# Batch 0's attention by pairs of tiles in a fused attention and expert kernel

## The chip, the cores and the metric

The kernel runs on one core of a Trainium2 chip. The metric is the device time of one execution in microseconds, the median of several runs. PE is the matrix engine, DVE the vector engine, ACT the scalar engine, POOL the GpSimd engine, SP the engine that issues most DMAs.

## The reference

Three layers follow each other. The attention has 2 batches, 8 heads, 576 positions and 64 columns a head; scores below the row's maximum less `tau` are masked:

```python
scores = scale * np.matmul(q, k.transpose(0, 1, 3, 2))
thresh = np.max(scores, axis=-1, keepdims=True) - tau
scores = np.where(scores >= thresh, scores, -1000000000.0)
scores = scores - np.max(scores, axis=-1, keepdims=True)
attn = np.exp(scores)
attn = attn / (np.sum(attn, axis=-1, keepdims=True) + 1e-09)
return np.matmul(attn, v).astype(np.float32)
```

Its output, as 1152 tokens of 512 columns, goes through `h = max(x @ w1, x @ w2, x @ w3)` and `h @ w_out` (the inner width is 768), and then through four experts of width 1024, each `relu(x @ w1[e]) @ w2[e]`, added up with normalised weights from `domain_probs`. The weights of the middle layer arrive as 64-bit floats, all else as 32-bit floats.

## The kernel before

All products are made in a 32-bit format of PE that keeps fewer bits, so each operand is split into a high part (a rounded copy, mostly on ACT) and a low part (the rest, on DVE or POOL), and two or three products are added up.

*Stages.* Batch 0's attention comes first (`attention_fast`, L408 to L473). The middle layer and the experts for the first 512 tokens follow (`layer_max(0)`, `experts(0)`), with batch 1's attention (`attention_slow`, L475) woven in from about 180 us; then the same layers for the other tokens. All their matmuls stand at L771.

*Tiles.* Batch 0 has four jobs, one for each pair of heads. Each job has nine tiles (`job_steps`, L208): four chunks of 128 query rows for either head, and one remainder tile with the 64 last rows of both heads. The two tiles of a chunk share a buffer `em` (L251), whose halves are the exponentials of either head; `st.mate` of the second tile is the first.

*One tile.* `qk` (L228) makes the scores with matmuls at L243 into a buffer of two PSUM banks; there are two such buffers. `peak` (L249) takes the negated maximum on DVE (L254). `limit` (L256) makes the threshold, one column on DVE (L257). `power` (L259) makes the exponential on ACT (L261). `weigh` (L263) masks it on DVE and adds it up at once (L266); this frees the score buffer. `norm` (L269) adds 1e-9 to the sum (L272), takes the reciprocal (L273), both one column on DVE, and scales the tile by it on POOL, for the last tiles on DVE (L274). `turn` (L280) transposes the tile on PE (L284, for some tiles L287 too). `cut_hi` (L307) and `cut_lo` (L323) split it: by turns with a second transposition on PE and a subtraction there (L330, L337, L338) or with a copy for POOL (L314, L334, L335), for remainders and the last tiles on DVE (L340). After half a job `gather` (L348) multiplies by the values (L360) and splits the result into X (L374, L377).

*Pipeline.* The loop of `attention_fast` goes tile by tile. In one turn tile i passes through `peak`, `power`, `limit` and `weigh`, tile i+1 through `qk`, tile i-1 through `norm` and `turn`, and tile i-2 through the splits. `advance` lets two queues make one step each: the preparation of the next job (`prep`, L130) and the value products.

*Order.* In batch 0's attention the order on each engine is not written out: a planner takes what is ready by its own times, earlier calls first. From the middle layer on, PE, DVE, ACT and POOL keep the order of the calls (`ORDER_B`, "pdas"). The first three weight blocks of the middle layer are prepared in the gaps of the attention (L584 to L604, then L564 and L568). `SWIFT` says for how many of the last tiles `norm` runs on DVE, `CALM` for how many the split is DVE's.

Of the kernel before, what the change touches and what calls it, by code (L numbers as in the profile page):

```python
# [14 lines left out]
ALU = mybir.AluOpType  # L15
# [6 lines left out]
def fused_kernel(ctx: ExitStack, tc: tile.TileContext, q, k, v, tau, w1, w2, w3, w_out, probs, m_w1, m_w2, out):  # L22
# [28 lines left out]
    LOAD, CUT = 1.5, 0.25  # L51
    AFTER = 1000
    EARLY = 3
    SWIFT = 2
    QUE0 = 3072
    QUE1 = 3072
    QUE2 = 10000
    CALM = 3
    DUP = nc.scalar.copy
    ORDER_A = ""  # L60
    ORDER_B = "pdas"
# [47 lines left out]
    def atile(shape, dt, tag):  # L109
        return at["pool"].tile(shape, dt, tag=tag, name=tag, bufs=at["bufs"].get(tag, 1))  # L110
# [138 lines left out]
    def peak(st):  # L249

        st.em = st.mate.em if st.mate else atile([P, 2 * S], F32, "em")  # L251
        st.col = (st.h or 0) * S
        st.stat = {x: atile([P, 1], F32, f"st_{x}") for x in ("negm", "thr", "sum", "r")}
        nc.vector.tensor_reduce(out=st.stat["negm"], in_=views(st)[0], op=ALU.max, axis=AX.XY, negate=True)  # L254

    def limit(st):  # L256
        nc.vector.tensor_scalar(out=st.stat["thr"], in0=st.stat["negm"], scalar1=-1.0, scalar2=ntau, op0=ALU.mult, op1=ALU.add)  # L257

    def power(st):  # L259
        sv, _, ev = views(st)  # L260
        nc.scalar.activation(out=ev, in_=sv, func=AF.Exp, bias=st.stat["negm"])  # L261

    def weigh(st):  # L263

        sv, _, ev = views(st)
        nc.vector.scalar_tensor_tensor(  # L266
            out=ev, in0=sv, scalar=st.stat["thr"], in1=ev, op0=ALU.is_ge, op1=ALU.mult, accum_out=st.stat["sum"])

    def norm(st, swift=False):  # L269
        em = views(st)[1]  # L270
        su, re = st.stat["sum"], st.stat["r"]
        nc.vector.tensor_scalar(out=su, in0=su, scalar1=1e-9, scalar2=None, op0=ALU.add)  # L272
        nc.vector.reciprocal(out=re, in_=su)  # L273
        last = (nc.vector if swift else nc.gpsimd).tensor_scalar(out=em, in0=em, scalar1=re, scalar2=even, op0=ALU.mult, op1=ALU.add)  # L274
        if st.h is None:
            nc.gpsimd.tensor_scalar(
                out=st.em[:, S:S + REM], in0=st.em[:, MAIN:S], scalar1=1.0, scalar2=1.0, op0=ALU.mult, op1=ALU.mult)
        return last
# [120 lines left out]
    def lined_up(jobs):  # L399
        steps = []  # L400
        for j, job in enumerate(jobs):
            new = job_steps(job)
            for r, st in enumerate(new):
                st.job, st.j, st.r = job, j, r
            steps += new
        return steps

    def attention_fast(jobs, modes):  # L408

        steps = lined_up(jobs)  # L410
        n = len(steps)
        front, back = Queue(), Queue()
        load_job(jobs[0])
        front.add(prep(jobs[0]))
        front.drain()
        back.add(values(jobs[0]))

        def advance():
            front.advance()
            back.advance()  # L420

        urgent = ExitStack()
        for i in range(n + 3):
            st = steps[i] if i < n else None
            nxt = steps[i + 1] if i + 1 < n else None
            old = steps[i - 2] if 0 <= i - 2 < n else None
            if st and st.j + 1 < len(jobs):
                if st.r == LOAD_A:
                    load_job(jobs[st.j + 1])
                if st.r == PREP_A:  # L430
                    front.add(prep(jobs[st.j + 1]))
            if i == 0:
                qk(st)
            if st:
                peak(st)
            if 0 <= i - 1 < n - 1:
                norm(steps[i - 1], i - 1 >= n - SWIFT)
            if nxt:
                if nxt.r == 0:
                    front.drain()  # L440
                    back.add(values(nxt.job))
                qk(nxt)
            if st and not nxt:
                power(st)
                limit(st)
                weigh(st)
                at["normed"] = norm(st, True)
                turn(steps[i - 1])
                urgent.enter_context(tc.issue_after(at["normed"].ins))
            if old:  # L450
                cut_hi(old, next(modes) if old.h is not None and i - 2 < n - CALM else "dve")
            advance()
            if nxt:
                power(st)
            if old:
                cut_lo(old)
            if nxt:
                limit(st)
            advance()
            if nxt:  # L460
                weigh(st)
                if i:
                    turn(steps[i - 1])
            if st and not nxt:
                at["turned"] = turn(st)
            if old:
                cut_late(old)
                if old.last:
                    back.add(gather(old.grp, i - 2 == n - 1))
            advance()  # L470
            yield
        back.drain()
        urgent.close()  # L473

    def attention_slow(jobs, modes):  # L475
# [12 lines left out]
        for i in range(n + 1):  # L488
# [30 lines left out]
            advance()  # L519
            yield  # L520
            if st:
                norm(st)
            if old:
                cut_lo(old)
# [386 lines left out]
```

## Time and profile before

| | |
|---|---|
| median of 3 runs | 750.08 us (749.97 to 750.29) |
| the profiled execution | 751.23 us |
| its span, first to last instruction | 749.4 us |
| mean granted TensorE clock | 1.000 |
| DMA, mean over the span | 92 GB/s |

The rows are read so. Times are in microseconds, means of one instruction in ns. PE is matmuls, PEld the weight loads that overlap them. A wait names the engine and line that waited, and the line whose end released it; idle time of an engine that does not set the pace costs nothing. Matmul ends are modelled, so that neighbours overlap in the listing.

### The profile page before, as it was taken

To read this page: it belongs to the slowest core of one execution; us is meant where nothing else is said; L and a number is where in the kernel's file an instruction comes from. 1 tells how busy PE (TensorE), PEld (TensorE's weight loads), DVE (VectorE), ACT (ScalarE), POOL (GpSimd) and SP (SyncE) were. 2 spreads that over 40 slices of the span, in tenths; PEclk is the share of its full clock that TensorE was granted. 3 is DMA by queue.
4 is the path that set the end of the run, shared out by engine and by line. 5 is a ranking of instruction groups with operands and counts; after the bars stand their busy time and mean duration, and the time that the engine had idled before them with its cause. 6 is when DMAs were issued, how large, how long until landed. Compare 5 with 4: busy or idle time off the path is not lost.

```text
span 749.4 us, 11712 instructions
## 1 busy us (share of the span) xinstructions
PE 714.0 (95%) x4103; PEld 634.9 (85%) x4103; DVE 378.6 (51%) x894; ACT 345.4 (46%) x740; POOL 396.2 (53%) x438
## 2 busy tenths in 40 slices
PE   3698999999999999999999999999999999999997
PEld 3587898777788788888888899999998998998996
DVE  3898897776365765766766421112222222222222
ACT  6598885445555555565464413324421321321320
POOL 5789884776755555564564525544623523522520
PEclk9999999999999999999999999999999999999999
DMA  6601004876723224122212233213412312312303
GB/s 184 197 18 33 0 2 126 277 229 211 194 84 90 58 70 118 57 73 57 84 58 65 77 113 86 67 54 92 128 56 84 96 46 85 106 44 77 113 2 71
DMA packets 81051, 68.95 MB, mean 92 GB/s; under 512 B 15840, under 2 KB 67040, under 8 KB 80992
## 3 DMA queue, kind: packets, MB, share of 16 engines
q1 hardware_dynamic: 80960, 68.19, 31.3%
q8 instruction: 33, 0.54, 0.3%
q14 instruction: 26, 0.21, 0.1%
q0 software_dynamic: 32, 0.00, 0.0%
HBM read 59.53 MB, written 8.65 MB: 91 GB/s over the span
## 4 chain that ended last, share of the span: by engine, by line
PE 77%; DVE 7%; POOL 4%; ACT 4%; issue 3%; DMA 3%; SPq 1%; POOLq 0%; ACTq 0%; DVEq 0%
PE ps L771 63%; PE u L360 4%; PE s L243 4%; PE t L284 3%; POOL a L568 2%; DVE st_negm L254 1%; DVE em L266 1%; ACT em L261 1%; DVE raw L604 1%; PE u L159 1%; DMA krem<-in_k_dram 1%; DMA words<-in_moe_w_dram 1%; ACT a L564 1%; POOL b L596 1%; DMA raw<-in_moe_w_dram 1%
## 5 line engine op out<-in xcount | busy, mean ns | idle before, releaser
L568 POOL TENSOR_TENSOR a<-raw,a 128x512 fp32r<-128x512 f32 (+1 forms) x116 | 145.3, 1259 | 162.8 <-ACT a L564 159.4
L771 PE MATMUL ps<-b,hh 128*128 128x512 f32 x576 | 184.4, 392 | 0.0
L771 PEld LDWEIGHTS ps<-b,hh 128*128 128x128 f32 x576 | 107.3, 188 | 20.6
L721 ACT ACTIVATE hh<-ps 128x320 fp32r<-128x320 f32 (+1 forms) x96 | 46.9, 489 | 151.1 <-PE ps L771 150.8
L771 PE MATMUL ps<-b,hl 128*128 128x512 f32 x288 | 113.1, 393 | 0.0
L771 PE MATMUL ps<-y1h,a 128*128 128x320 f32 x512 | 112.8, 309 | 0.0
L568 POOL TENSOR_TENSOR b<-raw,b 128x512 fp32r<-128x512 f32 x64 | 83.0, 1299 | 52.0 <-ACT b L564 52.0
L724 DVE SCALAR_TENSOR_TENSOR hl<-ps,hh 128x320 fp32r<-128x320 f32 (+1 forms) x96 | 53.5, 557 | 106.0 <-ACT hh L721 105.9
L564 ACT ACTIVATE a<-raw 128x512 fp32r<-128x512 f32 (+1 forms) x116 | 69.6, 612 | 58.6 <-PE ps L771 22.2
L740 DVE SCALAR_TENSOR_TENSOR acc<-ps,pr,acc 128x512 f32<-128x512 f32 x63 | 47.1, 748 | 80.4 <-PE ps L771 80.3
L261 ACT ACTIVATE em<-s,st_negm 128x576 f32<-128x576 f32 x72 | 53.5, 744 | 70.5 <-DVE st_negm L254 70.1
L771 PEld LDWEIGHTS ps<-y1h,a 128*128 128x128 f32 x512 | 85.7, 188 | 0.3
L771 PE MATMUL ps<-y0h,a 128*128 128x512 f32 x256 | 84.1, 399 | 1.2 <-POOL a L568 1.2
L274 POOL TENSOR_SCALAR em<-em,st_r,even 128x576 f32<-128x576 f32 x70 | 58.8, 841 | 47.0 <-DVE st_r L273 44.3
L771 PE MATMUL ps<-y1l,a 128*128 128x320 f32 x256 | 79.1, 309 | 0.0
L254 DVE TENSOR_REDUCE st_negm<-s 128x1 f32<-128x576 f32 x72 | 54.1, 753 | 48.8 <-PE s L243 48.4
L243 PE MATMUL s<-K,QS 128*128 128x288 f32 x320 | 59.5, 314 | 9.0 <-DVE em L266 8.4
L266 DVE SCALAR_TENSOR_TENSOR em<-s,st_thr,em 128x576 f32<-128x576 f32 x72 | 58.3, 812 | 11.9 <-ACT em L261 7.9
L771 PE MATMUL ps<-x1h,a 128*128 128x320 f32 x288 | 63.4, 309 | 0.0
L771 PEld LDWEIGHTS ps<-b,hl 128*128 128x128 f32 x288 | 54.1, 188 | 9.8
L243 PEld LDWEIGHTS s<-K,QS 128*128 128x128 f32 x320 | 49.6, 197 | 14.8 <-issue 7.0
L771 PEld LDWEIGHTS ps<-y0h,a 128*128 128x128 f32 x256 | 47.0, 188 | 9.9 <-POOL a L568 1.6
(109 smaller groups left out, 1280.5 us busy)
## 6 DMA issues: line engine op xcount, KB each, us to landing
raw<-in_moe_w_dram SPq DMA_DIRECT2D x128, 256.0 KB, 2.9
words<-in_moe_w_dram SPq DMA_DIRECT2D x18, 512.0 KB, 6.8
kept_w<-raw SPq DMA_DIRECT2D x18, 256.0 KB, 2.7
raw<-kept_w SPq DMA_DIRECT2D x18, 256.0 KB, 2.7
words<-in_moe_w_out_dram SPq DMA_DIRECT2D x8, 384.0 KB, 3.6
qraw<-in_q_dram SPq DMA_DIRECT2D x8, 256.0 KB, 3.5
kraw<-in_k_dram SPq DMA_DIRECT2D x16, 128.0 KB, 3.7
vraw<-in_v_dram SPq DMA_DIRECT2D x8, 256.0 KB, 3.7
```

The source lines that it names most:

```text
L243: nc.tensor.matmul(st.s[:, kh, 0:HS], lhsT=l, rhs=r, start=i == 0, stop=i == len(terms) - 1)
L254: nc.vector.tensor_reduce(out=st.stat["negm"], in_=views(st)[0], op=ALU.max, axis=AX.XY, negate=True)
L261: nc.scalar.activation(out=ev, in_=sv, func=AF.Exp, bias=st.stat["negm"])
L266: nc.vector.scalar_tensor_tensor(out=ev, in0=sv, scalar=st.stat["thr"], in1=ev, op0=ALU.is_ge, op1=ALU.mult, accum_out=st.stat["sum"])
L274: last = (nc.vector if swift else nc.gpsimd).tensor_scalar(out=em, in0=em, scalar1=re, scalar2=even, op0=ALU.mult, op1=ALU.add)
L360: at["valued"] = nc.tensor.matmul(pv, lhsT=l, rhs=r, start=i == 0, stop=i == len(terms) - 1)
L564: nc.scalar.activation(out=b["hi"], in_=b["raw"], func=AF.Copy)
L568: nc.gpsimd.tensor_tensor(out=b["lo"], in0=b["raw"], in1=f32(b["hi"]), op=ALU.subtract)
L721: nc.scalar.activation(out=hs[f][0][:, a:z], in_=ps, func=AF.Relu)
L724: nc.vector.scalar_tensor_tensor(out=hs[f][1][:, a:z], in0=ps, scalar=0.0, in1=f32(hs[f][0][:, a:z]), op0=ALU.max, op1=ALU.subtract)
L740: nc.vector.scalar_tensor_tensor(out=accs[t], in0=ps, scalar=pe, in1=accs[t], op0=ALU.mult, op1=ALU.add)
L771: nc.tensor.matmul(ps, lhsT=l, rhs=r, start=i == 0, stop=i == count - 1)
```

## The change

The loop goes by units: the two tiles of a chunk, or a remainder alone. The statistics of a pair lie in one tile of two columns. Both tiles of a unit pass through `peak` and `power`; one `limit` covers both columns; then `weigh` of either tile, mixed with `turn` and the splits of the unit before and with `qk` of the next unit; one `invert` (the sum and the reciprocal, taken out of `norm`) for both; then `norm` of either. `SWIFT` and `CALM` count units. `attention_slow` calls `invert` for each tile.

```diff
--- before.py
+++ after.py
@@ -51,11 +51,11 @@
     LOAD, CUT = 1.5, 0.25
     AFTER = 1000
     EARLY = 3
-    SWIFT = 2
+    SWIFT = 1
     QUE0 = 3072
     QUE1 = 3072
     QUE2 = 10000
-    CALM = 3
+    CALM = 2
     DUP = nc.scalar.copy
     ORDER_A = ""
     ORDER_B = "pdas"
@@ -250,11 +250,14 @@
 
         st.em = st.mate.em if st.mate else atile([P, 2 * S], F32, "em")
         st.col = (st.h or 0) * S
-        st.stat = {x: atile([P, 1], F32, f"st_{x}") for x in ("negm", "thr", "sum", "r")}
+
+        st.both = st.mate.both if st.mate else {x: atile([P, 2], F32, f"st_{x}") for x in ("negm", "thr", "sum", "r")}
+        st.stat = {x: t[:, st.h or 0:(st.h or 0) + 1] for x, t in st.both.items()}
         nc.vector.tensor_reduce(out=st.stat["negm"], in_=views(st)[0], op=ALU.max, axis=AX.XY, negate=True)
 
-    def limit(st):
-        nc.vector.tensor_scalar(out=st.stat["thr"], in0=st.stat["negm"], scalar1=-1.0, scalar2=ntau, op0=ALU.mult, op1=ALU.add)
+    def limit(st, both=False):
+        x = {nm: t[:, 0:2] for nm, t in st.both.items()} if both else st.stat
+        nc.vector.tensor_scalar(out=x["thr"], in0=x["negm"], scalar1=-1.0, scalar2=ntau, op0=ALU.mult, op1=ALU.add)
 
     def power(st):
         sv, _, ev = views(st)
@@ -266,11 +269,14 @@
         nc.vector.scalar_tensor_tensor(
             out=ev, in0=sv, scalar=st.stat["thr"], in1=ev, op0=ALU.is_ge, op1=ALU.mult, accum_out=st.stat["sum"])
 
+    def invert(st, both=False):
+        x = {nm: t[:, 0:2] for nm, t in st.both.items()} if both else st.stat
+        nc.vector.tensor_scalar(out=x["sum"], in0=x["sum"], scalar1=1e-9, scalar2=None, op0=ALU.add)
+        nc.vector.reciprocal(out=x["r"], in_=x["sum"])
+
     def norm(st, swift=False):
         em = views(st)[1]
-        su, re = st.stat["sum"], st.stat["r"]
-        nc.vector.tensor_scalar(out=su, in0=su, scalar1=1e-9, scalar2=None, op0=ALU.add)
-        nc.vector.reciprocal(out=re, in_=su)
+        re = st.stat["r"]
         last = (nc.vector if swift else nc.gpsimd).tensor_scalar(out=em, in0=em, scalar1=re, scalar2=even, op0=ALU.mult, op1=ALU.add)
         if st.h is None:
             nc.gpsimd.tensor_scalar(
@@ -407,8 +413,13 @@
 
     def attention_fast(jobs, modes):
 
-        steps = lined_up(jobs)
-        n = len(steps)
+        units = []
+        for st in lined_up(jobs):
+            if st.mate:
+                units[-1].append(st)
+            else:
+                units.append([st])
+        n = len(units)
         front, back = Queue(), Queue()
         load_job(jobs[0])
         front.add(prep(jobs[0]))
@@ -419,55 +430,53 @@
             front.advance()
             back.advance()
 
+        def begin(st):
+            if st.r == 0:
+                front.drain()
+                if st.j:
+                    back.add(values(st.job))
+            qk(st)
+
         urgent = ExitStack()
-        for i in range(n + 3):
-            st = steps[i] if i < n else None
-            nxt = steps[i + 1] if i + 1 < n else None
-            old = steps[i - 2] if 0 <= i - 2 < n else None
-            if st and st.j + 1 < len(jobs):
-                if st.r == LOAD_A:
-                    load_job(jobs[st.j + 1])
-                if st.r == PREP_A:
-                    front.add(prep(jobs[st.j + 1]))
-            if i == 0:
-                qk(st)
-            if st:
+        for st in units[0]:
+            begin(st)
+        for i in range(n + 1):
+            new = units[i] if i < n else []
+            nxt = units[i + 1] if i + 1 < n else []
+            old = units[i - 1] if i else []
+            for st in new:
+                if st.j + 1 < len(jobs):
+                    if st.r == LOAD_A:
+                        load_job(jobs[st.j + 1])
+                    if st.r == PREP_A:
+                        front.add(prep(jobs[st.j + 1]))
                 peak(st)
-            if 0 <= i - 1 < n - 1:
-                norm(steps[i - 1], i - 1 >= n - SWIFT)
-            if nxt:
-                if nxt.r == 0:
-                    front.drain()
-                    back.add(values(nxt.job))
-                qk(nxt)
-            if st and not nxt:
                 power(st)
-                limit(st)
-                weigh(st)
-                at["normed"] = norm(st, True)
-                turn(steps[i - 1])
+                advance()
+            if new:
+                limit(new[0], len(new) == 2)
+            for k in range(2):
+                if k < len(old):
+                    at["turned"] = turn(old[k])
+                    cut_hi(old[k], next(modes) if old[k].h is not None and i - 1 < n - CALM else "dve")
+                advance()
+                if k < len(new):
+                    weigh(new[k])
+                if k < len(nxt):
+                    begin(nxt[k])
+                if k < len(old):
+                    cut_lo(old[k])
+                    cut_late(old[k])
+                    if old[k].last:
+                        back.add(gather(old[k].grp, i == n))
+                advance()
+            if new:
+                invert(new[0], len(new) == 2)
+            for st in new:
+                at["normed"] = norm(st, i >= n - SWIFT)
+                advance()
+            if i == n - 1:
                 urgent.enter_context(tc.issue_after(at["normed"].ins))
-            if old:
-                cut_hi(old, next(modes) if old.h is not None and i - 2 < n - CALM else "dve")
-            advance()
-            if nxt:
-                power(st)
-            if old:
-                cut_lo(old)
-            if nxt:
-                limit(st)
-            advance()
-            if nxt:
-                weigh(st)
-                if i:
-                    turn(steps[i - 1])
-            if st and not nxt:
-                at["turned"] = turn(st)
-            if old:
-                cut_late(old)
-                if old.last:
-                    back.add(gather(old.grp, i - 2 == n - 1))
-            advance()
             yield
         back.drain()
         urgent.close()
@@ -519,6 +528,7 @@
             advance()
             yield
             if st:
+                invert(st)
                 norm(st)
             if old:
                 cut_lo(old)
```

## Rows read from the trace of the kernel before

**Rows 1.** Busy us by stage: engines, granted clock, DMA share, GB/s.
```profile
13.00:40.00 27.00, 17.04 (x95) 14.81 (x94) 23.68 (x61) 18.82 (x43) 19.32 (x25) 1.00 0.61 179
40.00:118.50 78.50, 71.74 (x533) 65.44 (x533) 69.20 (x228) 66.89 (x153) 64.56 (x90) 1.00 0.05 13
118.50:180.00 61.50, 58.08 (x280) 47.65 (x279) 48.47 (x85) 30.59 (x60) 44.08 (x49) 1.00 0.73 229
```

**Rows 2.** PE's waits from 13 to 40 us: total, times, longest.
```profile
PE s L243 <- DVE em L266: 7.2, 4, 3.6
```

**Rows 3.** PE's waits from 40 to 118.5 us.
```profile
PE t L284 <- POOL em L274: 2.2, 4, 1.0
PE s L243 <- DVE em L266: 1.2, 2, 0.9
PE t L284 <- ACT am L338: 1.0, 1, 1.0
```

**Rows 4.** PE's waits from 118.5 to 200 us.
```profile
PE ps L771 <- POOL a L568: 3.1, 5, 1.2
```

**Rows 5.** Groups by line and shape, 0 to 118.5 us: busy, mean ns, idle before.
```profile
L266 DVE SCALAR_TENSOR_TENSOR em<-s,st_thr,em 128x576 f32<-128x576 f32 x36 | 29.0, 811 | 5.9 <-ACT em L261 3.3 <-POOL K L179 1.6 <-POOL VR L197 0.6
L274 POOL TENSOR_SCALAR em<-em,st_r,even 128x576 f32<-128x576 f32 x34 | 29.0, 854 | 9.7 <-DVE st_r L273 7.1 <-DVE st_thr L257 1.8 <-PE t L284 0.5
...
L254 DVE TENSOR_REDUCE st_negm<-s 128x1 f32<-128x576 f32 x36 | 26.8, 748 | 2.1 <-PE s L243 1.8
...
L257 DVE TENSOR_SCALAR st_thr<-st_negm,ntau 128x1 f32<-128x1 f32 x36 | 7.1, 204 | 0.2
...
L273 DVE RECIPROCAL st_r<-st_sum 128x1 f32<-128x1 f32 x36 | 5.5, 153 | 0.2
...
L272 DVE TENSOR_SCALAR st_sum<-st_sum 128x1 f32<-128x1 f32 x36 | 5.2, 144 | 0.3
...
L266 DVE DVE_READ_ACCUMULATOR em<-s,st_thr,em 128x1 f32 x36 | 2.9, 82 | 0.0
...
L342 DVE TENSOR_TENSOR ar<-u,ar 64x64 fp32r<-64x64 f32 x8 | 1.7, 217 | 0.1
```

**Rows 6.** DVE in order of time: start us, duration us, line, operation.
```profile
87.70 0.14 DVE L272 TENSOR_SCALAR st_sum<-st_sum 128x1 f32<-128x1 f32 x1
87.77 0.81 DVE L266 SCALAR_TENSOR_TENSOR em<-s,st_thr,em 128x576 f32<-128x576 f32 x1
...
93.08 0.21 DVE L257 TENSOR_SCALAR st_thr<-st_negm,ntau 128x1 f32<-128x1 f32 x1
93.20 0.15 DVE L273 RECIPROCAL st_r<-st_sum 128x1 f32<-128x1 f32 x1
93.27 0.41 DVE L340 TENSOR_TENSOR am<-t,am 128x256 fp32r<-128x256 f32 x1
```

**Rows 7.** L257 alone by stretch: DVE busy us and count.
```profile
13.00:40.00 27.00, 1.76 (x9) 1.00 0.61 179
40.00:109.00 69.00, 5.11 (x27) 1.00 0.05 14
```

**Rows 8.** All engines in order of time, the end of the attention stage.
```profile
108.51 0.78 PE L243 MATMUL s<-K,QS 128*128 128x288 f32 x4
...
113.07 0.58 DVE L274 TENSOR_SCALAR em<-em,st_r,even 128x576 f32<-128x576 f32 x1
...
115.00 0.60 PE L284 MATMUL t<-ident,em 128*128 128x128 f32 x4
...
118.22 0.31 PE L360 MATMUL u<-ar,VR 128*128 128x320 f32 x1
```

**Rows 9.** L243 alone by stretch: PE and weight-load busy us.
```profile
40.00:109.00 69.00, 21.71 (x119) 16.77 (x120) 1.00 0.05 14
```

**Rows 10.** L243 in the stage: duration ns least, median, greatest.
```profile
L243 PE MATMUL s<-K,QS x160: 289/295/607, 11.4 to 109.0; 128*128 128x288 f32 x160
```

## The prediction

> **What bounds the kernel now.** I read the table by stage first [rows 1]. The reader is to see three stretches. From 13 to 40 us DVE is busy 23.68 of 27.00 us and PE only 17.04. From 40 to 118.5 us, the rest of batch 0's attention, PE is busy 71.74 of 78.50 us and DVE (69.20), ACT (66.89) and POOL (64.56) follow closely: PE sets the pace there, but no engine has much room. After 118.5 us come the dense layers, where PE is busy 58.08 of 61.50 us in the first part. So the change, which touches only what happens before 118.5 us, can win at most what PE idles there.
>
> Next I read who ends PE's idle time. Between 13 and 40 us it is above all DVE: the score matmuls at L243 wait 7.2 us for `weigh` (L266) to free a score buffer [rows 2]. Between 40 and 118.5 us the listed waits come to 6.6 us: 2.2 us for `norm` on POOL, 1.2 us for `weigh`, and 3.2 us in six smaller items, the greatest 1.0 us, for ACT and others that the change does not speed up [rows 3]. So 3.4 of 6.6 us, about half, hang on the DVE chain and the `norm` behind it.
>
> Last I looked at what comes after: the greatest of PE's waits from 118.5 to 200 us, 3.1 us, is for split weights on POOL [rows 4]. Order on PE, DVE, ACT and POOL is written out there, so that stage starts when attention lets go of the engines.
>
> **The small instructions.** Batch 0 has 36 tiles: 32 in 16 pairs and 4 remainders. Each tile has one L257, one L272 and one L273, 36 of each, with means of 204, 144 and 153 ns [rows 5]. A pair now issues one of each, so 16 of each kind go, 48 in all. By recorded durations that is 16 x (204 + 144 + 153) ns = 8.0 us. But these records overlap their followers: an L272 starts at 87.70 us and the next DVE instruction at 87.77; an L273 at 93.20 and the next at 93.27; an L257 at 93.08 and the next at 93.20 [rows 6]. By these distances one of each costs 0.07 + 0.07 + 0.12 = 0.26 us, and the 48 cost 4.2 us of DVE time. I take 4.2, because what the follower can use is the distance between starts, and keep 8.0 for the end of the range. Where the follower needs the result the full duration counts, so the truth lies between.
>
> The Trainium skill ("VectorE: DVE Perf Modes", section "The DRAIN you can't avoid") says that the next VectorE instruction does not start until the pipe has emptied, and its rules for kernel authors advise to cut the number of instructions. The trace does not agree with the strict form: a recorded 0.14 us stood for 0.07 us of issue in the row above. By the strict form the saving would be the 8.0 us; that case is a rival below.
>
> No row shows these three on two columns. The nearest wider row is L342 on 64 columns, 217 ns [rows 5]: about what L257 takes on one column, so at the near end a second column costs nothing; at the far end it costs the 73 ns by which L342 exceeds L272, and the 60 instructions that are left (20 units, three each) would give back 4.4 us. I take nothing.
>
> **Where the saving lands.** Of the 36 L257, 9 lie between 13 and 40 us and the others after it [rows 7]. A quarter of 4.2 us is 1.05 us in the first stretch, where PE waits for DVE; DVE is busy 88% of it, so I count 0.9 us. Three quarters, 3.15 us, fall where PE is the pace; of the waits about half hang on this chain, so I count half, 1.6 us. The other half only makes DVE idle longer.
>
> **What the pair adds as waits.** (1) The threshold of tile 0 now waits for the maximum of tile 1 (0.75 us), and `norm` of tile 0 for `weigh` of tile 1 (0.81 + 0.08 us) [rows 5]. Behind the waiting threshold DVE holds both `weigh`; behind these PE holds the next score matmuls, since there are two score buffers and the pair takes both. The loop through one buffer is: two maxima 1.50, threshold 0.20, first `weigh` 0.89, score matmuls 0.78 [rows 5, 8], together 3.37 us. In the stage a pair takes 69.0 / 27 x 2 = 5.1 us [rows 7], so 1.7 us are left for DVE's other work (splits and sums of other tiles) before this loop is the pace. The exponential of tile 0 is hidden behind the maximum of tile 1, that of tile 1 behind the first `weigh`. While DVE goes round, PE has 71.74 - 21.71 = 50.0 us of other work [rows 1, 9] over some 28 tiles, 3.6 us a pair, against a hole of 1.84 us (maximum of tile 1, threshold, `weigh`) between the second score product and the next first. On average that covers it. (2) POOL does two `norm` in a row, and the turns come one unit later, behind the next pair's maxima; PE waited for `norm` four times already (2.2 us) [rows 3]. Growing each by 0.89 us would be 3.6 us; I take 0.3, since the new place of the turns leaves at least the two maxima (1.5 us) for POOL's two `norm` of 0.85 us [rows 5]. Below nothing is possible too: four waits less are -2.2.
>
> **The end of the stage.** In the last two tiles nothing of substance changes but the pairing: both are normalised on DVE and split on DVE before and after (two tiles or one unit; the third from last is a remainder, which is always split there). Now the last `norm` ends at 113.65 us and its turn begins at 115.00, held by matmuls ahead of it on PE [rows 8]. That is 1.35 us of cover for a pair's delay of about 0.9 us (the first `weigh` behind the last maximum). I take 0.2; without the cover it is 0.9.
>
> **The rest.** Batch 1's attention issues the same instructions as before; only their columns lie in a shared tile: nothing. Loads and preparation are called a little earlier in a unit: their DMAs stay far from the limit between 40 and 118.5 us (DMA share 0.05 [rows 1]), nothing, up to 0.5 either way at the start, where the share is 0.61. From 118.5 us on I pass on the whole gain, since the written order there just starts earlier; at least 0.7 of it would pass if the weight chain, which makes PE wait 3.1 us, held its own time.
>
> **Sum.** -0.9 - 1.6 + 0.3 + 0.2 = -2.0 us. The profiled execution took 751.23 us (749.4 span and 1.83 around it), so a profiled one would take 749.2; the median of the runs, 750.08, lies 1.15 us lower, and the same step from there is **748.1 us**. With the bounds (half the saving, or none lost to pairing) this case's own range is 746.5 to 749.3.
>
> **Rivals.**
> (a) *The pair starves PE* (slower). The hole of 1.84 us must be filled by turns in pairs that have no value product (L360) beside them. Two turns and a second transposition are at most 3 x 0.60 us [rows 8], 1.8 us, and DVE's other work can stretch the hole by up to the 1.7 us left above. That is a bubble of nothing to 1.7 us on the 8 pairs without a value product, up to 14 us; at 0.8 us each it is 6.4, less the 2.5 saved, +3.9: 754.0 us. It decides once the hole grows past some 2.1 us, where 8 bubbles of 0.3 us eat the 2.5 us. For it: PE already waited for `weigh`, up to 0.9 us at a time, after 40 us [rows 3]. Against: the average cover is twice the hole.
> (b) *No change.* DVE is not the pace after 40 us; the saving becomes DVE idle time and only the first stretch gains, 0.9 less 0.5: 749.7 us. For it: the 6.6 us of waits are spread over POOL, ACT and DVE. Against: half of them end with the chain that gets shorter.
> (c) *The full durations count*: 8.0 us, a quarter of it (2.0) and half of the rest (3.0) less 0.5: -4.5, 745.6 us. The strict rule of the Trainium skill above would bring this; the starts 0.07 us apart speak against it.
> (d) *The columns are not independent*: the second maximum, which writes the tile that the first exponential reads, waits for it (0.75 us [rows 5]) in all 16 pairs, half of it hidden: +6 - 2 = 754 us. The halves of `em` already are written by different engines side by side, so I give it little.
> (e) *The new order disturbs the start*: weight conversion fills DVE gaps there, and PE's score products take up to 607 ns there against 295 in the median, at a granted clock of 1.00 [rows 1, 10], so that its first matmuls may quicken earlier or later: 2 us either way.
>
> **How the numbers follow.** Likeliest case 0.45, (a) 0.20, (b) 0.17, (c) 0.10, (d) 0.04, (e) 0.04. The time is the likeliest's. About 0.2% (1.5 us) is what can be told from no change, so faster is below 748.6. Faster: four fifths of the likeliest, (c), half of (e) and a little of (b): 0.50. Within: 0.24. Slower: (a), (d) and half of (e): 0.26. The range runs from 745.0, which holds (c), to 753.0, which leaves out the upper half of (a) and (d).
>
> **What would show it.** 20 of each small instruction before the stage ends; the last value product (L360, now ending at 118.5 us [rows 8]) about 2 us earlier, nearly half of it by 40 us; PE waits on `norm` and `weigh` together below 3.4 us. Rival (a) shows as L243 waiting for L266 by well over 1.2 us after 40 us; (b) as DVE idle up and PE idle unchanged; (d) as second maxima waiting for ACT. The prediction is wrong if the stage ends later, or if it ends earlier and the waits on L568 after it grow by as much.

## The result and the profile after

The changed kernel took **756.2 us** (median of 4 runs, 754.54 to 757.24) against 750.1 us (749.97 to 750.29): ratio 1.0079, 95% interval 1.0062 to 1.0095. It is slower by about 5.9 us where the prediction had 2.0 us faster. The 5.9 us are the ratio's; the medians are 6.1 us apart. The profiled execution of after is its shortest run, 754.54 us with a span of 752.8 us, and that of the kernel before took 751.23 us, longer than any of its four runs here, so the rows below hold 3.3 us of the loss.

The table by stage for after, with the columns of [rows 1]:

```profile
13.00:40.00 27.00, 17.71 (x97) 14.82 (x96) 23.40 (x50) 19.59 (x46) 20.84 (x27) 0.94 0.63 184
40.00:118.50 78.50, 68.23 (x497) 60.97 (x498) 69.95 (x183) 63.09 (x145) 63.02 (x87) 1.00 0.03 9
118.50:180.00 61.50, 57.92 (x288) 48.09 (x289) 48.12 (x84) 30.92 (x61) 41.65 (x46) 1.00 0.71 215
```

Two things stand here. From 40 to 118.5 us PE does 3.5 us less work than before (68.23 against 71.74). And DVE, which lost 48 instructions, is no less busy: 69.95 us against 69.20. The groups by line and shape, 0 to 122 us, tell why [rows 5]:

```profile
L269 DVE SCALAR_TENSOR_TENSOR em<-s,st_thr,em 128x576 f32<-128x576 f32 x36 | 28.7, 815 | 3.4 <-ACT em L264 2.0
L280 POOL TENSOR_SCALAR em<-em,st_r,even 128x576 f32<-128x576 f32 x34 | 28.2, 838 | 8.4 <-DVE st_r L275 6.9 <-PE t L290 0.9 <-PE u L168 0.5
L260 DVE TENSOR_SCALAR st_thr<-st_negm,ntau 128x2 f32<-128x2 f32 x16 | 7.2, 449 | 0.3
L274 DVE TENSOR_SCALAR st_sum<-st_sum 128x2 f32<-128x2 f32 x16 | 5.7, 357 | 0.2
L275 DVE RECIPROCAL st_r<-st_sum 128x2 f32<-128x2 f32 x16 | 2.6, 160 | 0.3
```

The reciprocal of two columns costs what that of one did (160 against 153 ns). The threshold went from 204 to 449 ns and the sum from 144 to 357 ns: 32 instructions take 12.9 us where 32 narrow ones took 5.6. Merging removed 48 records and made 32 of the others 7.3 us longer in all.

The timeline of after shows what they wait for (start us, duration us, engine, line, operation, idle time before):

```profile
91.58 1.29 POOL L341 TENSOR_TENSOR am<-tcopy,am 128x512 fp32r<-128x512 f32 x1
91.76 1.14 DVE L274 TENSOR_SCALAR st_sum<-st_sum 128x2 f32<-128x2 f32 x1
92.93 0.17 DVE L275 RECIPROCAL st_r<-st_sum 128x2 f32<-128x2 f32 x1
93.20 1.63 POOL L280 TENSOR_SCALAR em<-em,st_r,even 128x576 f32<-128x576 f32 x2 [0.33 <-DVE st_r L275]
94.08 0.66 PE L290 MATMUL t<-ident,em 128*128 128x128 f32 x4 [1.17 <-POOL em L280]
```

The sum starts while POOL's L341 runs and ends at 92.90 us, 0.03 us after L341 does (92.87). Of its 1.14 us the `norm` loses little: POOL was busy with L341 until 92.87 us in any case and then sat idle for 0.33 us before the `norm`, so no more than 0.33 of the 1.17 us that PE waits here can be the hold's. What the hold takes for certain is time of DVE.

The hold shows nearly throughout. Of the 16 two-column sums, the eight that began with POOL idle took 0.15 to 0.17 us; of the eight begun while POOL ran, seven ended 0.02 to 0.03 us after POOL's instruction and took 0.28 to 1.14 us, and the eighth began 0.01 us before POOL's ended. Of the 16 two-column thresholds thirteen ended 0.02 to 0.03 us after an instruction of POOL; one, at 100.18 us, took 0.23 us while a `norm` that POOL had begun 0.08 us before it ran on for another 0.53 us. In the kernel before, one-column ones that began while POOL ran took 0.19 to 0.22 us (threshold) and 0.14 to 0.15 us (sum), no longer than the others. No semaphore asks for the wait, and the profile counts it as busy time.

The Trainium skill ("SBUF — State Buffer", section "Who interferes with whom") says that VectorE and GpSimd share one pair of ports into SBUF, that a `tensor_scalar` can enter a two-port mode, and that the second to start is then blocked until the first is done. This trace agrees, with the ends above, but for that one threshold. The prediction did not draw on it.

PE's waits in after, from 13 to 40 us [rows 2]:

```profile
PE u L149 <- ACT kraw L138: 3.3, 1, 3.3
PE u L293 <- DVE K L176: 2.2, 1, 2.2
PE s L243 <- DVE em L269: 1.5, 1, 1.5
```

From 40 to 118.5 us [rows 3]:

```profile
PE t L290 <- POOL em L280: 4.0, 5, 1.2
PE s L243 <- DVE em L269: 1.2, 3, 0.6
PE t L290 <- DVE em L280: 0.9, 1, 0.9
```

And from 118.5 to 200 us [rows 4]:

```profile
PE ps L781 <- POOL a L578: 2.3, 5, 0.5
```

In the first stretch the wait for `weigh` fell as foreseen, from 7.2 to 1.5 us, and waits of the next job's preparation (L149, L293) took its place. After 40 us the scores wait for `weigh` no more than before (1.2 us); the turns wait for `norm` twice as long (4.0 against 2.2 us, and 0.9 us for the last one on DVE). The dense layers give back 0.8 us.

The end of the stage in after [rows 8]:

```profile
111.64 0.80 PE L243 MATMUL s<-K,QS 128*128 128x288 f32 x4
...
116.82 1.53 DVE L280 TENSOR_SCALAR em<-em,st_r,even 128x576 f32<-128x576 f32 x2
117.60 0.63 PE L290 MATMUL t<-ident,em 128*128 128x128 f32 x4 [0.90 <-DVE em L280]
...
122.53 0.31 PE L366 MATMUL u<-ar,VR 128*128 128x320 f32 x1
```

The last score matmuls start at 111.64 us instead of 108.51, 3.1 us late, and the last value product ends at 122.84 instead of 118.53: the tail adds 1.2 us to what was lost ahead of it. Where it was lost shows in PE's busy time in three stretches of the stage (window, length, busy us, count, granted clock, DMA share, GB/s), for the kernel before:

```profile
20.00:40.00 20.00, 13.32 (x82) 1.00 0.56 166
40.00:90.00 50.00, 44.83 (x334) 1.00 0.07 19
90.00:118.50 28.50, 26.91 (x202) 1.00 0.01 2
```

and for after:

```profile
20.00:40.00 20.00, 14.46 (x86) 0.91 0.60 180
40.00:90.00 50.00, 44.48 (x328) 1.00 0.05 13
90.00:118.50 28.50, 23.75 (x171) 1.00 0.01 1
```

Until 90 us after is level; in the last 28.5 us it does 31 matmul records less. The last matmul of a job's preparation starts at 88.0 us in the kernel before and at 87.1 us in after, so in those 28.5 us no preparation fills PE's gaps.

### The profile page after: what moved, and what is told of

It is laid out like the page before. It is cut to its first block, busy times and chain, and to the rows that moved or that the text cites. A ratio compares the mean times of both kernels' runs of the same rounds, so it can differ in the third digit from the quotient of the medians.

```text
span 752.8 us, 11646 instructions
## 1 busy us (share of the span) xinstructions
PE 715.5 (95%) x4103; PEld 634.7 (84%) x4103; DVE 382.7 (51%) x846; ACT 345.1 (46%) x740; POOL 396.7 (53%) x438
## 4 chain that ended last, share of the span: by engine, by line
PE 75%; DVE 10%; POOL 4%; issue 4%; ACT 3%; DMA 2%; SPq 0%; DVEq 0%; POOLq 0%; ACTq 0%
PE ps L781 63%; PE u L366 4%; PE s L243 4%; PE t L290 2%; DVE st_negm L256 2%; DVE em L269 2%; POOL a L578 2%; DMA words<-in_moe_w_dram 1%; DMA kraw<-in_k_dram 1%; PE u L159 1%; DVE raw L614 1%; POOL b L606 1%; DVE x L371 1%; ACT a L574 1%; ACT em L264 1%
## 5 line engine op out<-in xcount | busy, mean ns | idle before, releaser
L243 PE MATMUL s<-K,QS 128*128 128x288 f32 x320 | 59.1, 314 | 3.3 <-DVE em L269 2.7
L243 PEld LDWEIGHTS s<-K,QS 128*128 128x128 f32 x320 | 49.8, 198 | 8.7 <-DVE em L269 4.6
```

The costliest lines, as they stand in the source:

```text
L243: nc.tensor.matmul(st.s[:, kh, 0:HS], lhsT=l, rhs=r, start=i == 0, stop=i == len(terms) - 1)
```

## The experiments

Two theories to begin with. **A**: the two-column `tensor_scalar`, held by POOL, costs the time. **B**: working in pairs, or the new order of work that comes with it, costs it. All ratios are to the kernel before, run on the same chip beside them. Where "order fixed" is said, the order of the instructions on every engine is written out as that of the changed kernel; elsewhere the planner makes an order of its own, and that need not be the order of the calls.

**e2_wide.** The kernel before, tile by tile, in nearly its own order (13 of 4103 matmul records stand elsewhere in its trace), with threshold and sum on two columns; the second is a dummy.

```
-out=st.stat["thr"], in0=st.stat["negm"]   # [P, 1]
+out=st.wide["thr"], in0=st.wide["negm"]   # [P, 2]; the sum likewise
```

> The kernel before, tile by tile, but threshold and sum work on two columns (the second is a dummy that nothing reads), 72 instructions. Theory A: each is held by 0.23 us in the mean as in the changed kernel, 16 us of DVE time, half of it on the path: 754 to 762 us. Theory B: nothing that starves PE is added, 750 to 751.

Measured: 760.01 us, ratio 1.0127 [1.0114, 1.0141]. Its two groups, and its stage from 40 to 118.5 us:

```profile
L269 DVE TENSOR_SCALAR rg_thr<-rg_negm,ntau 128x2 f32<-128x2 f32 x36 | 20.1, 567 | 0.2
L285 DVE TENSOR_SCALAR rg_sum<-rg_sum 128x2 f32<-128x2 f32 x36 | 12.3, 341 | 0.3
```

```profile
40.00:118.50 78.50, 67.66 (x486) 59.58 (x485) 75.41 (x209) 63.55 (x143) 61.01 (x86) 1.00 0.05 12
```

Width alone, with no instruction merged and no pair, costs 9.5 us: DVE goes from 69.20 to 75.41 us and PE loses 4.1 us of work, as theory A had it. The hold costs time here.

**p1_narrow, p3_all, p4_reduce.** The changed kernel, order fixed, with the hold taken away: p1 makes threshold and sum per tile (32 instructions more), p3 the reciprocal too (48 more), p4 keeps one instruction per pair but makes threshold and sum as `tensor_reduce` over a value and a constant.

```
-limit(new[0], len(new) == 2)          # p1, p3: one column each
+for st in new: limit(st)
-tensor_scalar(out=thr[:, 0:2], ...)   # p4
+tensor_reduce(out=thr[:, 0:2], in_=(negm, -ntau)[:, 0:2, :], op=add, negate=True)
```

> The first round mixed two things, since the planner made a new order for each kernel. Here every engine keeps the order of the changed kernel, instruction for instruction (written out as edges between neighbours); only the threshold and the sum of a pair are two one-column instructions, one behind the other. Theory A (the hold of the two-column form is on the path): 3 to 6 us below the changed kernel's 756.2, 750 to 753 us. Theory B (the order and the pairing cost the time, the hold is hidden): 755 to 757.

> As the one before, and the reciprocal too one column at a time: the small instructions of the kernel before in the order of the changed one. Theory A: within 0.7 us of the one before, as 16 reciprocals of 0.16 us come back. If the number of small instructions were the lever, 2 us slower.

> The order of the changed kernel and as many small instructions as it has, but threshold and sum as reductions over value and constant (0.15 us each before). Theory A: as p1_narrow or up to 1 us faster. Theory B: 755 to 757. If the width of two columns costs, slower than p1_narrow by 3 or more.

Measured: 754.59 us, 1.0066 [1.0053, 1.0079]; 754.67, 1.0058 [1.0046, 1.007]; 753.87, 1.0052 [1.0037, 1.0068]. The groups of p4 that took the place of the two held ones, and its reciprocal:

```profile
L294 DVE RECIPROCAL st_r<-st_den 128x2 f32<-128x2 f32 x16 | 2.6, 161 | 0.3
L276 DVE TENSOR_REDUCE st_thr<-rg_negm 128x2 f32<-128x4 f32 x16 | 2.4, 151 | 0.2
L293 DVE TENSOR_REDUCE st_den<-rg_sum 128x2 f32<-128x4 f32 x16 | 2.4, 148 | 0.2
```

Reductions of two columns are not held (151 and 148 ns). But all three kernels stay 4 to 5 us above the kernel before; p1 lies between the ranges of its two theories. At the changed kernel's order the hold is worth 1.0 to 2.0 us (the ratios from 1.0079 down to 1.0066 and 1.0052; their intervals still overlap, but q1 below, held as after is and in the same order, comes out at 1.008 too). Theory A explains about a third of the loss at most. And p3 and p4, with 48 instructions between them, are 0.5 us apart by their ratios, less than the intervals. What is left belongs to the fixed order, with the pairing in it: in p3's trace the first threshold of a pair stands behind the second maximum in all 16 pairs.

**q1_three.** The changed kernel, order fixed, three columns instead of two (the third a dummy).

```
-x = {nm: t[:, 0:2] ...}
+x = {nm: t[:, 0:3] ...}
```

> This is the changed kernel in its own order on every engine, with three columns instead of two in the merged thresholds, sums and reciprocals; the third column is a dummy. Theory A1 (an even number of columns lets the one-source tensor_scalar take the second pair of ports, which GpSimd's running instruction holds; an odd number does not): both go back to 0.14 to 0.21 us whatever GpSimd runs, and the time is that of p4_reduce, 752.5 to 755. Rival A2 (any tensor_scalar on more than one column waits for GpSimd): means of 0.35 to 0.45 us again, and 755 to 757.

Measured: 755.95 us, 1.008 [1.0067, 1.0094].

```profile
L273 DVE TENSOR_SCALAR rg_thr<-rg_negm,ntau 128x3 f32<-128x3 f32 x16 | 7.4, 465 | 0.2
L287 DVE TENSOR_SCALAR rg_sum<-rg_sum 128x3 f32<-128x3 f32 x16 | 5.7, 358 | 0.2
```

Rival A2 holds: an odd width is held too, as long as two, and the time is that of after. The Trainium skill ("VectorE: DVE Perf Modes", section "What auto-detection actually checks") asks that the outermost dimensions of source and destination be either both even or equal. Theory A1 rested on the first half of that alone; three columns to three columns are equal, and these rows agree with the whole.

**v1_nosum.** The kernel before in its own order on every engine, without the 36 instructions of batch 0 that add 1e-9 to the sum.

```
-nc.vector.tensor_scalar(out=su, in0=su, scalar1=1e-9, ...)   # batch 0
```

> This is the kernel before, in its own order on every engine, without the 36 instructions of batch 0 that add 1e-9 to the sum (the reciprocal reads the bare sum). It prices a small instruction taken out of the tile-by-tile loop. If VectorE's loop through the score buffers sets the pace everywhere, 36 x 0.144 = 5.2 us go: 744.9. If they count at 0.09 us each, in the half of the stretch that is VectorE's, as the prediction had it, 1.6 to 3.2 us go: 747 to 748.5. If they stand off the path: 750, no change.

Measured: 750.12 us, 0.9995 [0.9986, 1.0005]. Its stages:

```profile
13.00:40.00 27.00, 17.07 (x96) 14.90 (x95) 23.28 (x53) 18.80 (x43) 19.51 (x26) 1.00 0.60 172
40.00:118.50 78.50, 71.77 (x534) 65.52 (x533) 67.42 (x198) 67.04 (x154) 64.14 (x89) 1.00 0.05 12
```

DVE is less busy by 0.4 and 1.8 us than in [rows 1] and PE does the same work, 71.77 us. A sum taken out of the tile-by-tile loop is worth nothing here, or by the interval at most 1 us for all 36. The thresholds, which stand ahead of `weigh`, were not taken out by themselves; p3 and p4 differ in 16 of them and in 32 others, and are no further apart than their intervals. So even without the hold there is no sign of the saving that the change is after.

**e1_narrow, e3_order, e4_reduce, p5_soon.** The calls in pairs once more, with the planner free. e1 has threshold and sum per tile and the reciprocal merged; e3 has everything per tile; e4 is p4 without the fixed order. p5 is p3 (order fixed) with sum and reciprocal of a pair's first tile moved ahead of the second `weigh`.

> The pair order is kept; the threshold and the sum are made one column at a time, two instructions for a pair, and only the reciprocal covers both columns. Theory A (a two-column tensor_scalar is held until POOL's running instruction ends; the 32 of them took 12.9 us where 32 one-column ones take 5.6): 7.3 us of DVE time come back, two thirds of it on the path, 749 to 751 us, and the rows of both lines read 0.14 to 0.21 us. Theory B (the pair takes both score buffers and starves PE): unchanged, 754 to 757. Theory C (PE's clock falls in the gap near 25 to 30 us): between them, and 1.00 or not in the granted clock from 30 to 35 us decides.

> The pair order alone: threshold, sum and reciprocal one column at a time, the same 108 instructions as before. Theory A: at 749 to 752 us, near the kernel before. Theory B: 754 to 757, as the changed kernel.

> The pair order with one instruction a pair, but the threshold and the sum are made by tensor_reduce over two columns each (value and constant, the constants written once), not by tensor_scalar. Theory A (held only in the form that tensor_scalar takes on two columns): 747 to 750 us, no row of the two lines over 0.3 us. If width alone cost (any two-column instruction), 754 to 757 and rows as long as in the changed kernel. Theory B: 754 to 757 with short rows.

> As p3_all, but sum and reciprocal of a pair's first tile stand right behind its weigh, so that its norm on POOL need not wait for the second tile's weigh (0.9 us). If that wait is what the pairing costs, 1 to 3 us below p3_all; if PE waits for other things, within 0.5 us of it.

Measured: e1 756.94 us, 1.0089 [1.0071, 1.0107]; e3 753.04, 1.0034 [1.0021, 1.0046]; e4 756.39, 1.0076 [1.0064, 1.0088]; p5 756.95, 1.0091 [1.0078, 1.0104]. e1 and e3 differ in code by 16 reciprocals, and by 3.9 us; with the order fixed the same edit (p1 against p3) moves 0.1 us. So the order that the planner finds can be worth some 4 us, more than any instruction in question. Nor is it the order of the calls: in e3's trace the first threshold of a pair stands behind the second maximum in 3 of 16 pairs, in the kernel before in 6. With nothing on two columns the planner takes the pairs apart, so e3 tests the rewritten calls and not the pairs; its time lies between its two theories. e1 has the time of theory B, and so has e4, where the reductions on two columns hold the pairs together.

In p5 the two instructions between the two `weigh` put the second one 0.27 us later in the mean and cost 2.3 us, where neither of its cases had a loss. From 40 to 118.5 us PE's wait for `weigh` rises from 0.3 us in p3 to 1.1 us, and that for `norm` on POOL falls from 2.9 to 2.5 us: in this order what follows `weigh`, the next score matmuls, counts for more than the `norm`.

**x1_last, x2_single, x3_late.** Theory B in parts, on e3: x1 calls the last job's tiles singly, x2 all tiles, x3 calls the next job's preparation one pair later.

```
-if st.mate:
+if st.mate and st.j < len(jobs) - 1:   # x1;  x2: if False:
-PREP_A = 1
+PREP_A = 3                             # x3
```

> This is e3_order (pairs, every small instruction for one tile, 753.04 us) in which the nine tiles of the last job are worked one at a time by the same loop instead of in pairs; TensorE's program is that of e3_order, only VectorE's order of the last job differs. Theory B1 (the pair costs in the last job and the tail, where no next job fills TensorE, because both tiles' sums and norms stand behind both weighs): the 600th to 650th matmul come as early as in the kernel before, and the time is 750.0 to 751.5. Theory B2 (the pair costs wherever it stands, or it is the rewritten loop's order of TensorE's program): 752.5 to 753.5, no change.

> This is e3_order with no pairs at all: the rewritten loop runs over single tiles, every small instruction for one tile. If working in pairs is what costs (theories B1 and B2's first half), it is at the kernel before, 749.5 to 751. If it is the rewritten loop (the turn of a tile one place later or earlier among the other work, the scores begun behind the weigh), it stays above: 752 to 755.

> This is e3_order with the preparation of the next job called at its fourth tile (the second pair) instead of its second (the first pair). Theory C (the pair order leaves TensorE idle at 25 to 35 us, behind transposes of the second job's keys that wait for their DMA and ScalarE, and the lower granted clock there costs): the granted clock of 30 to 40 us stays at 1.00, some ten matmuls more are done by 40 us, and the time is 751 to 752.5. Theory B (the start is made up later): 753 to 755, since the preparation is then pushed closer to the end of its job.

Measured: x1 753.38 us, 1.0042 [1.0028, 1.0056]; x2 757.16, 1.0093 [1.0079, 1.0107]; x3 754.0, 1.005 [1.0036, 1.0065]. In x1's trace all four engines run the very order of e3, which had taken the pairs apart already, so x1 decides nothing about the last job. x3 is where theory B had it. x2 is slower than even the second of its two cases. Its stages, and PE alone in two stretches:

```profile
13.00:40.00 27.00, 17.27 (x83) 14.84 (x82) 22.59 (x58) 18.58 (x43) 18.25 (x25) 0.88 0.61 179
40.00:118.50 78.50, 69.17 (x514) 62.76 (x513) 66.84 (x220) 64.74 (x147) 63.48 (x88) 1.00 0.05 12
```

```profile
40.00:90.00 50.00, 42.88 (x315) 1.00 0.07 19
90.00:118.50 28.50, 26.28 (x201) 1.00 0.01 2
```

The rewritten loop without pairs, with the same narrow instructions as before, is as slow as the changed kernel: PE does 2.6 us less after 40 us though DVE is less busy than in [rows 1]. So a loss of this size needs no pairs; the calls of the rewritten loop and the planner's order are enough. But it is not the changed kernel's loss. x2 is behind by 12 matmul records at 40 us and loses 19 more by 90 us, and after that it keeps up (201 records against 202), where the changed kernel loses its 31 after 90 us and p3, in the same order without the hold, 21:

```profile
90.00:118.50 28.50, 25.21 (x181) 1.00 0.01 2
```

What the pairs themselves cost in the order of the changed kernel is therefore not shown.

**z2_cuts, z6_pace, z7_pace_cuts, y2_pace.** The diff changes two things in that order. **Depth**: the cuts of a tile stood two tiles behind its scores (`old = steps[i - 2]`) and now stand straight behind its turn, one unit behind. **Pace**: `advance()`, which moves on the preparation of the next job, the values and the gathers, was called 3 times a tile and is called 8 times a pair, 6 times a single tile. z2 undoes the depth in x2, z6 the pace, z7 both; y2 undoes the pace in e3 (a remainder keeps five calls).

```
-turn(old); cut_hi(old); ... cut_lo(old); cut_late(old)         # old = units[i - 1]
+cut_hi(done); ... cut_lo(done); turn(old); cut_late(done)      # z2, z7: done = units[i - 2]
-for k in range(2): ... advance() ... advance()
+for k in range(max(len(new), len(old))): ...                   # y2, z6; z7: range(1)
-    at["normed"] = norm(st, ...); advance()
+    at["normed"] = norm(st, ...)                               # y2, z6, z7
```

> This is x2_single (the rewritten loop over single tiles, 757.16 us) with the cuts of a tile two tiles behind its scores, as in the kernel before, instead of one. Theory D (depth: the rewritten loop has the cut straight behind its transposes, one unit behind the scores, so nothing slack stands between a norm, its transposes and its cut): it comes back to 750 to 752. Theory F (pace: the rewritten loop lets the preparation of the next job, the values and the gathers advance 6 times a tile, in a pair 4 times a tile, instead of 3, so their transposes get in front of the scores and wait for DMA and ScalarE): no change, 755 to 758.

> This is x2_single with three advances of the side queues a tile, as in the kernel before, instead of six, and the cuts one tile behind. Theory F (pace): 750 to 752, and the granted clock at 20 to 40 us stays at 1.00. Theory D (depth): no change, 755 to 758.

> This is x2_single with both: cuts two tiles behind and three advances a tile. Its order on every engine is that of the kernel before but for 14 of 4107 lines of TensorE and 24 of 826 of VectorE. If depth and pace are all that the rewritten loop changed for single tiles: 749.5 to 751. If it stays above 753, the cause is in neither.

> This is e3_order (pairs, small instructions for one tile, 753.04 us) with three advances of the side queues a tile instead of four. Theory F: what pace costs in pairs goes, 750 to 751.5, and the dip of the granted clock at 20 to 40 us goes too. Theory D (in pairs the cut must follow its transposes at once, since a pair holds both transpose banks): no change, 752 to 754.

Measured: z2 751.14 us, 1.0015 [1.0004, 1.0025]; z6 751.54, 1.0023 [1.0014, 1.0033]; z7 751.35, 1.0017 [1.0009, 1.0026]; y2 752.55, 1.0043 [1.0027, 1.0059]. For single tiles either one alone takes back most of the 7.0 us (5.9 the depth, 5.3 the pace), and both together no more. z7 has the order of the kernel before but for a few lines, so the two together make up what x2 lost. Which of them does it is not shown: the theory of depth had z6 unchanged and that of pace z2, and both came back. x2, z2 and z6 each run an order that the planner made anew, and such orders can differ by some 4 us by themselves (e1 and e3).

y2 against e3 changes nothing that can be told, but e3 runs few tiles in pairs, so this says little of the pace in pairs. The depth was not undone in pairs: the two turns of a pair take both transposition banks, so its cuts must follow at once. z7 still stands 1.2 us above the kernel before, and that is not settled further; in the profiled executions its stage ends as early (118.48 us against 118.53), and the spans are level (749.5 and 749.4 us).

**q2_three_pace.** q1 at the pace of y2, with the planner free.

> This is q1_three with three advances of the side queues a tile, in the order that comes of it (not fixed), so the pair with merged instructions, without the hold if theory A1 holds, and at the pace of y2_pace (752.55 us). If 48 instructions fewer are worth what the prediction gave them, 2.5 us less than y2_pace: 750. If they are worth nothing, as v1_nosum showed for 36: 752 to 753.5. The order differs from that of y2_pace, which alone can move it by 2 us or more.

Measured: 763.7 us, 1.0196 [1.0173, 1.022], slower than either theory had it. Held instructions (means of 463 ns for the threshold and 474 ns for the sum, to the end of its stage at 135 us) and a new order act together here, and its profile has a granted clock of 0.91 from 40 to 118.5 us; how much is whose was not taken apart.

No version beats the kernel before: v1_nosum is level with it and leaves work out.

## Why the prediction was wrong

**"At the near end a second column costs nothing ... I take nothing": failed.** It measured +245 ns for the threshold and +213 ns for the sum, in the mean. The far end, 73 ns from L342 of 64 columns, was too low as well: that row is another operation and reads PSUM, so it could not show the hold, and no narrow `tensor_scalar` of more than one column stood among the rows. The reciprocal alone came out as forecast. DVE's saving of 4.2 us did not happen (69.20 to 69.95 us after 40 us); the hold cost 1.0 to 2.0 us of the end time on top.

**"Half of it, 1.6 us" where PE is the pace, and 0.9 us in the first stretch: not borne out even without the hold.** v1_nosum took 36 of the 108 away, the sums, and won nothing. That a wait ends with a chain does not make each of the chain's instructions worth its time: from 13 to 122 us PE waited 8.4 us for `weigh` and 2.2 us for `norm` in the kernel before, and 8.2 and 2.1 us in v1_nosum, with 36 instructions less ahead of them.

**"Loads and preparation are called a little earlier in a unit ... nothing": the costly omission.** Four to five of the 5.9 us are left when the hold is gone (p1, p3, p4), and belong to the new order, with the pairing in it. The prediction counted how many instructions wait behind which maximum; it did not count that a cut now follows its turn at once, nor that `advance()` goes from 6 to 8 a pair. In single tiles undoing either brought 5 to 6 us, but x2 lost its time at another place than the changed kernel did. Which part of the new order costs the 4 to 5 us in the changed kernel (depth, pace, or the pairing itself) stays open; the records say that it is lost after 90 us.

**"I take 0.3" for the turns behind `norm`:** PE's wait for `norm` grew by 1.8 us on POOL and 0.9 us on DVE (2.2 to 4.0, and the 0.9 new). With the hold gone (p3) it is still 2.9 and 0.9 us. The two maxima were no cover: in the timeline above POOL is still at a split (L341) when the sum starts, and PE waits 1.17 us for the `norm` behind both.

**"I take 0.2" at the end:** the tail is 1.2 us longer, above the 0.9 us given for a cover that is gone.

**Rival (a)** has a time, 754.0 us, that is nearer than the forecast, but not the mechanism: its mark, scores waiting for `weigh` by well over 1.2 us after 40 us, did not come (1.2 us again). **Rival (b)**, no gain from DVE after 40 us, is what v1_nosum shows for the sums alone. **Rival (c)** falls with the saving. **Rival (d)** did not come: of the 5.3 us that DVE sat idle before the maxima, 5.2 us ended with PE's scores and none of note with ACT. **Rival (e)** shows no part: after is level with before at 40 us (97 matmul records from 13 us on against 95). Its reading of [rows 10], 607 ns "at a granted clock of 1.00", was wrong: those matmuls ran at the lower level of the clock, as the last section shows.

**The range.** Its lower bound, 746.5 us, does not come out of "none lost to pairing", which gives 750.08 - 2.5 = 747.6 us.

**What held:** the 20 instructions of each kind, and the wait for `weigh` in the first stretch falling (7.2 to 1.5 us). Nothing was gained by it, since PE then waited for the preparation of the next job (3.3 and 2.2 us).

## What to carry to other kernels

Before two small `tensor_scalar` are merged into a wider one, look at what GpSimd runs beside them: in these traces they didn't meet it on one column, on two or three most of those that began beside it ended when its instruction ended, and a reduction or a reciprocal of the same width took no longer. Where PE is the pace, price a saving on another engine by taking the instruction out of the old order, not by its duration. Read a rewritten loop for distance and pace (how many tiles between a product and its reader, how often side queues move) before counting its instructions. And where a planner orders the work, see in the trace which order ran before a result is put down to the calls: e3 was called in pairs and ran few, and x1 was an edit that changed nothing.

## What the runs showed of the hardware

The hold is invisible as a wait: DVE counts as busy for up to 1.32 us with a two-column threshold whose shortest record takes 0.22 us, and for up to 1.14 us with a two-column sum whose shortest takes 0.15 us.

In after the clock falls when PE has idled. PE is busy 1.43 of 5.00 us from 25 to 30 us; from 29.9 to 33.3 us it gets the lower of its two levels (1.2 GHz, against 2.4), which makes 0.67 in the mean of the next 5 us:

```profile
25.00:30.00 5.00, 1.43 (x8) 0.99 0.81 237
30.00:35.00 5.00, 4.08 (x20) 0.67 0.57 172
```

At the lower level four score matmuls take 1.31 us, at the higher 0.78 us (the row of 108.51 us in [rows 8]). By that measure the kernel before ran its start at the lower level, though the table prints 1.00 there:

```profile
31.51 1.31 PE L243 MATMUL s<-K,QS 128*128 128x288 f32 x4
...
20.96 1.30 PE L243 MATMUL s<-K,QS 128*128 128x288 f32 x4 [0.67 <-DVE em L266]
...
34.93 0.79 PE L243 MATMUL s<-K,QS 128*128 128x288 f32 x4 [0.17 <-DVE em L266]
```

The first row is of after, the others of the kernel before, whose four at 25.83 us take 1.30 us and whose four at 29.53 us 0.77 us. Its trace holds no record of the clock before 29.52 us, and the view counts such time as 1.00. So its 1.00 from 13 to 40 us is not a higher clock than the 0.94 of after, or than the 0.59 that z6_pace shows from 20 to 30 us; z6_pace ends its stage within 0.4 us of the kernel before.
